# Attention's sums of a head: order of their products and their place ahead of the scores

## The chip, the core and the metric

The kernel runs on one core of one Trainium2 chip. The metric is the device time of one execution in microseconds. Engines are named as the profile names them: PE (TensorE matmuls), PEld (its weight loads), DVE (VectorE), ACT (ScalarE), POOL (GpSimd) and SP (SyncE, which issues the transfers). Each engine executes its own instructions in the order in which the built program has them, and waits for others by semaphores.

## What is computed

The reference is one block: a conditioned layer norm, attention with a compressive memory over four segments of 512 tokens, a second conditioned layer norm, and a token-mixing MLP. Attention, cut to what matters here, for each of 32 heads of 32 numbers:

```
for s in range(4):                       # segments of 512 tokens
    logits = qs @ ks.T * 32**-0.5 + causal_mask
    p = softmax(logits)
    a_dot = p @ vs
    a_mem = (phi(qs) @ M) / (phi(qs) @ z + 1e-6)
    o = g * a_mem + (1 - g) * a_dot
    M += phi(ks).T @ vs ; z += sum(phi(ks))
```

with `g = sigmoid(beta)`. Then `x + ga * (o @ wo)`, the norm, and the MLP over the token axis. All is in float32.

## The kernel before, in words

Float32 accuracy comes from splitting numbers into a first part (rounded) and a second part (the rest), and multiplying parts: a projection has three products for each pair of tiles.

Attention goes over 32 **units** (line 364): two passes, in each eight groups of four heads, in each two segments. A unit has four heads, so there are 128 heads in this count; number n is unit n // 4, head n % 4. For a unit:

- `project` (line 380) makes keys, values and queries (tiles `nps`, lines 188 to 197, and `qps`, lines 199 to 203), transposes keys (`kps`, line 415) and sends the split operands of each head to the tiles `sk` by SP's transfers.
- `memory` (line 446) reads the compressive memory (`rd`, line 455) and updates it (`up`, line 465).
- `maxima(t, h)` (line 473) computes scores in three matmul groups `sx`, `sy`, `sz` (line 483) into two banks, takes row maxima on DVE (line 485), and after each second head transposes them (`nmps`, line 491); four small transfers (line 498) put them as rows into `sk`.
- `scores(t, h)` (line 512) computes transposed scores, less the maxima, in four matmuls `a0`, `a1`, `a2` (two; lines 519, 522, 525, 526) into two banks. ACT takes the exponential of each bank (lines 520, 523, 527) into `p32`, of which there are two buffers. POOL masks the diagonal blocks (line 530), ACT rounds all 1280 columns to float16 as the probabilities' **first part** (line 532), and POOL subtracts it from `p32` in two halves of 640 columns, which gives the **second part** (line 534). Both parts lie in `ph`, of which there are two buffers.
- `values(t, h)` (line 536) sums over keys: ten products with the first part, 97 columns wide, then ten with the second part, 65 wide, all into the one bank `pv` (line 548). DVE takes the reciprocal of the row sums (551), adds the three column groups (553) and scales (555); POOL adds the memory's part in all but the first segment (558). After the fourth head PE transposes the unit's result (`ops`, line 563), ACT copies it out and SP stores it.

The loop at line 690 emits, for step n, the scores of head n, the maxima of head n + 3, the sums of head n - 1, a piece of the projection eight steps ahead, and planned work of other kinds. This is not the order that runs: the program is built with a scheduler (line 1138) that places the instructions of each engine by its own timing estimate, with the order of emission as their priority. Which instruction of PE follows which is therefore a result of the build. PE's order was read off the built programs before and after.

`norm_all` (line 214) normalizes four token tiles, twice at the start. Its means, variances and factors lie in a small tile `mv4` of 20 numbers for each partition. `csb` (line 104) holds the condition vector `c` and its sigmoid, 16 numbers for each partition, and is not read after line 110.

Of the kernel before, what the change touches and what calls it, by code (L numbers as in the profile page):

```python
# [7 lines left out]
F32 = mybir.dt.float32  # L8
# [10 lines left out]
P = 128  # L19
# [8 lines left out]
NV = 97  # L28
# [3 lines left out]
VL = 1  # L32
# [12 lines left out]
def attention_and_mlp(ctx, tc, x, wq, wkv, wo, beta, w1, b1, w2, b2, c, wm_a, wm_b, out):  # L45
# [19 lines left out]
    a = par.__enter__()  # L65
    scb, gaw = (a.tile([P, D], F32, name=n) for n in ("scb", "gaw"))
    acst_pool = tc.tile_pool(name="acst", bufs=1)
    acst = acst_pool.__enter__()
# [6 lines left out]
    def bank(tag, bufs, name):  # L75
        return psum.tile([P, 512], F32, tag=tag, bufs=bufs, name=name)
# [27 lines left out]
    csb = acst.tile([P, 2, NK], F32, name="csb")  # L104
# [39 lines left out]
    def new_page(name):  # L144
        return page.tile([P, 2, 512], F32R, tag="page", bufs=16, name=name)
# [32 lines left out]
    def load_w(g, pr):  # L178
        res = W[pr, g] = {}
        for kind, part in (("v", 0), ("v", 1), ("q", 0)):  # L180
            load_part(g, pr, kind, part, res)
        if pr == 0:
            keep_w(g)
# [30 lines left out]
    def norm_all(tiles):  # L214

        with tc.high_priority():
            m = acst.tile([P, 5, 4], F32, tag="mv4", bufs=1, name="mv4")
            r, t, nb = m[:, 2], m[:, 3], m[:, 4]
            mv = m[:, 0:2].rearrange("p a b -> p (a b)").rearrange("p (i a) -> p i a", a=2)
            for k, src in enumerate(tiles):  # L220
                st = const.tile([P, 2, 6], F32, tag="st", bufs=4, name="st")
                for i in range(2):
                    V.bn_stats(st[:, i], src[:, 512 * i:512 * i + 512])
                last_stats = V.bn_aggr(mv[:, k], st)
            A.activation(r, mv[:, :, 1], AF.Ln, bias=eps)
            exp = A.activation(r, r, AF.Exp, scale=-0.5)
            V.scalar_tensor_tensor(t, mv[:, :, 1], EPS, r, op0=ALU.add, op1=ALU.mult)
            V.scalar_tensor_tensor(t, t, -0.5, r, op0=ALU.mult, op1=ALU.mult)
            V.scalar_tensor_tensor(r, t, 1.5, r, op0=ALU.add, op1=ALU.mult)
            V.scalar_tensor_tensor(nb, mv[:, :, 0], -1.0, r, op0=ALU.mult, op1=ALU.mult)  # L230
            for k, src in enumerate(tiles):
                if k % 2:
                    last_v = V.tensor_scalar(src, src, r[:, k:k + 1], nb[:, k:k + 1], op0=ALU.mult, op1=ALU.add)
                else:
                    last_a = A.activation(src, src, AF.Identity, scale=r[:, k:k + 1], bias=nb[:, k:k + 1])
        return last_stats, exp, last_a, last_v
# [85 lines left out]
    for i in range(2):  # L322
        ps = bank("s2", 2, f"scps{i}")
        for j in range(4):
            T.transpose(ps[:, 128 * j:128 * j + 128], bc[:, 4 * i + j], ident)
        A.copy(scb[:, 512 * i:512 * i + 512], ps)
    last_stats = norm_all(xs[0])[0]
    srow.append(scale_row(1))
    for cb in range(2):
# [16 lines left out]
    b = late.__enter__()  # L346
# [12 lines left out]
    def reload_h(seg, ct):  # L359
        pg = new_page(f"h{seg}_{ct}")  # L360
        SY.dma_start(pg.bitcast(F32), hT1[seg - 2, ct])
        hpages[seg, ct] = pg
# [140 lines left out]
    @contextmanager  # L503
    def behind(n, engines):

        with ExitStack() as s:
            for e in engines:
                if (n, e) in marks:
                    s.enter_context(tc.issue_after(marks[n, e].ins))
            yield  # L510
# [25 lines left out]
    def values(t, h):  # L536
        pr, g, seg = its[t]
        d = st[t]
        am, ph = d["am"], d["ph", h]
        pv = bank("pv", 1, f"pv{t}_{h}").rearrange("p (a n) -> p a n", a=4)  # L540
        col = {0: lambda i: 128 * i, 1: lambda i: 512 + 128 * (i - 1), 2: lambda i: 1024 + 128 * (i - 2),
               3: lambda i: 896}
        n = 0
        for part, w in ((0, NV), (1, 65)):
            for i in range(4):
                for j in range(i + 1):
                    o = col[j](i)
                    T.matmul(pv[:, i, 0:w], ph[:, part, o:o + 128], d["vp"][:, j, h, 0:w], start=(n == 0),  # L548
                             stop=(n == 19), skip_group_check=True)
                    n += 1  # L550
        V.reciprocal(pv[:, :, 0], pv[:, :, 0])
        red = r_.tile([P, 4, 32], F32, tag="red", bufs=2, name=f"red{t}_{h}")
        V.tensor_reduce(red, pv[:, :, 1:97].rearrange("p a (c e) -> p a e c", c=3), axis=AX.X, op=ALU.add)
        ah = am[:, :, 32 * h:32 * h + 32]
        V.scalar_tensor_tensor(red if seg else ah, red, gate[:, 1, 4 * g + h:4 * g + h + 1],  # L555
                               pv[:, :, 0:1].to_broadcast([P, 4, 32]), op0=ALU.mult, op1=ALU.mult)
        if seg:
            G.tensor_tensor(ah, ah, red, op=ALU.add)
        if h < 3:
            return  # L560
        ps = bank("ms", 1, f"ops{t}")
        for i in range(4):
            T.transpose(ps[:, 128 * i:128 * i + 128], am[:, i], ident)
        ot = r_.tile([P, L], F32, tag="ot", bufs=1, name=f"ot{t}")
        A.copy(ot, ps)
        SY.dma_start(oT[g, :, L * seg:L * seg + L], ot)
        del st[t]
# [29 lines left out]
    def at(f, n):  # L597
        if 0 <= n < 4 * NI:
            f(n // 4, n % 4)
# [3 lines left out]
    def seg_load(seg):  # L603
        seg_x[seg] = [load_x(s2p, tt) for tt in range(4 * seg, 4 * seg + 4)]
        return norm_all(seg_x[seg])
# [69 lines left out]
    for g in range(2, NG):  # L675
        n = 8 * g - 13
# [5 lines left out]
    for j in range(32):  # L682
        n = ML0 + MLS * j
        later(n, lambda j=j: mod_fetch(j), n + 2, lambda r, j=j: mod_late(j, r), "V")
    plan(WO0 - 3, lambda: spread(gaw, 0))
    for i in range(8):
        n = WO0 + WOS * i
        later(n, lambda i=i: wo_fetch(i), n + 2, lambda r, i=i: wo_split(i, r), "G")

    for n in range(-LEADS, 4 * NI + VL):  # L690
        at(scores, n)
        at(maxima, n + LEADS)
        at(values, n - VL)
        m = n + LEADP
        if 0 <= m + 4 < 4 * NI:
            t = (m + 4) // 4
            if its[t][:2] not in W:
                with tc.issue_after(last_sk[0, 3].ins):
                    load_w(its[t][1], its[t][0])
        if m >= 8:  # L700
            at(project, m)
        if 59 <= m < 67:
            seg, ct = 2 + (m - 59) // 4, 2 * ((m - 59) % 4)
            reload_h(seg, ct)
            reload_h(seg, ct + 1)
        if 4 * NI - 5 <= m < 4 * NI + 3:
            i = m - 4 * NI + 5
            for c in (2 * (i % 4), 2 * (i % 4) + 1):
                wop[c, i // 4] = new_page(f"wo{c}_{i // 4}")
                if c < 5 or i < 4:  # L710
                    SY.dma_start(wop[c, i // 4].bitcast(F32), wos[c, i // 4])
        for f, engines in todo.pop(n, ()):
            with behind(n, engines):
                f()
# [14 lines left out]
    w = cw_pool.__enter__()  # L729
# [412 lines left out]
```

## Time and profile before

| | |
|---|---|
| median of 3 runs | 2239.49 us (2235.74 to 2240.94) |
| the profiled execution's own time | 2239.78 us |
| its span in the profile | 2238.1 us |
| DVE, ACT busy | 75%, 51% of the span |
| DMA | 423.05 MB, 189 GB/s in the mean |

The span runs from the first to the last profiled instruction of the program. A busy share is the union of an engine's instructions over the span; PE's matmuls overlap each other, so their durations are longer than the distance from one start to the next, and a price for PE's time has to be taken from the distances. In the grouped view a row gives line, engine, operation, tiles and shapes, the count, busy us and mean ns, then the engine's idle time just before and what ended it.

### The profile page before, as it was taken

What the parts mean: (1) busy time and instruction counts of PE and PEld (TensorE: products, weight loads), DVE (VectorE), ACT (ScalarE), POOL (GpSimd) and SP (SyncE); (2) the same over time, 40 slices, a digit from 0 to 9 for tenths busy, and PEclk for the clock granted to TensorE, in tenths of its full rate; (3) what the DMA queues carried; (4) which work ended last, traced back from release to release, by engine and by line L of the source; (5) the groups of instructions that cost most, each with busy time, mean ns of one, the idle gap of its engine ahead of it and who ended that gap; (6) DMA issues with size and microseconds to landing.
All of it is one profiled execution on the core that took longest, in us unless ns stands there. A gap on an engine that the chain in (4) does not pass through costs nothing.

```text
span 2238.1 us, 38277 instructions
## 1 busy us (share of the span) xinstructions
PE 2199.5 (98%) x13786; PEld 1888.4 (84%) x13786; DVE 1679.5 (75%) x3762; ACT 1137.1 (51%) x2082; POOL 731.0 (33%) x831
## 2 busy tenths in 40 slices
PE   8999999998999999999999999999999999999999
PEld 5889898888999899988888888888888888888887
DVE  7677677766777777655758766888888896869687
ACT  5477777665666666655546633533334242424232
POOL 2176656656777676654001200033330000000000
PEclk9999999999999999999999999999999999999999
DMA  7556565687566565665664587655556541414134
GB/s 285 189 175 206 162 188 156 182 298 239 158 195 194 159 202 181 197 185 181 230 209 154 224 324 264 257 206 224 205 201 235 201 147 58 155 57 146 57 123 151
DMA packets 175185, 423.05 MB, mean 189 GB/s; under 512 B 17524, under 2 KB 71828, under 8 KB 166036
## 3 DMA queue, kind: packets, MB, share of 16 engines
q1 hardware_dynamic: 174996, 420.61, 56.8%
q8 instruction: 109, 1.79, 0.3%
q14 instruction: 80, 0.66, 0.1%
HBM read 244.62 MB, written 125.06 MB: 165 GB/s over the span
## 4 chain that ended last, share of the span: by engine, by line
PE 85%; DMA 4%; POOL 3%; DVE 3%; ACT 3%; issue 2%; SPq 1%; ACTq 0%; DVEq 0%; POOLq 0%
PE mx L922 48%; PE nps L195 10%; PE po L792 8%; PE qps L203 7%; PE pv L548 3%; POOL ph L534 2%; PE a L519 1%; PE sz L483 1%; PE sx L483 1%; DMA sk<-sg 1%; ACT ph L532 1%; PE a L522 1%; DVE wv L125 1%; DMA sk<-nt 1%; PE srow L296 1%
## 5 line engine op out<-in xcount | busy, mean ns | idle before, releaser
L922 PE MATMUL mx<-bU,sp 128*128 128x512 f32 x2352 | 534.4, 389 | 0.9 <-DVE ac L929 0.9
L922 PEld LDWEIGHTS mx<-bU,sp 128*128 128x128 f32 x2352 | 441.3, 188 | 93.5 <-issue 1.3
L195 PE MATMUL nps<-wv,h 128*128 128x256 f32 x3072 | 441.7, 283 | 1.2 <-DVE h L125 0.5
L534 POOL TENSOR_TENSOR ph<-p,ph 128x640 f16<-128x640 f32 x256 | 382.3, 1514 | 157.1 <-ACT ph L532 154.2
L122 ACT CAST sp<-wr 128x384 fp32r<-128x384 f32 (+2 forms) x408 | 217.0, 545 | 423.6 <-PE mx L922 352.1
L922 PE MATMUL mx<-bA,sp 128*128 128x512 f32 x1764 | 430.5, 389 | 0.0
L195 PEld LDWEIGHTS nps<-wv,h 128*128 128x128 f32 x3072 | 407.1, 189 | 8.8 <-DVE h L125 2.0
L922 PEld LDWEIGHTS mx<-bA,sp 128*128 128x128 f32 x1764 | 331.2, 188 | 68.6
L125 DVE TENSOR_TENSOR sp<-wr,sp 128x384 fp32r<-128x384 f32 (+2 forms) x408 | 259.6, 647 | 28.6 <-ACT sp L122 28.4
L929 DVE TENSOR_TENSOR ac<-mx,ac 128x512 f32<-128x512 f32 x280 | 189.4, 685 | 84.1 <-PE mx L922 83.1
L203 PE MATMUL qps<-h,wq 128*128 128x512 f32 x768 | 201.7, 403 | 0.2
L532 ACT CAST ph<-p 128x1280 f16<-128x1280 f32 x128 | 161.3, 1260 | 42.6 <-POOL p L530 42.1
L792 PE MATMUL po<-wo,ots 128*128 128x512 f32 x768 | 179.4, 390 | 0.0
L792 PEld LDWEIGHTS po<-wo,ots 128*128 128x128 f32 x768 | 143.3, 188 | 29.0 <-DVE x L795 0.2
L203 PEld LDWEIGHTS qps<-h,wq 128*128 128x128 f32 x768 | 141.9, 191 | 29.5 <-ACT vp L406 0.9
L922 PE MATMUL mx<-bB,sp 128*128 128x512 f32 x588 | 164.0, 389 | 0.0
L530 POOL TENSOR_SCALAR_AFFINE_SELECT p<-p 128x256 f32<-128x256 f32 x256 | 123.5, 493 | 99.7 <-ACT p L527 51.6
L548 PE MATMUL pv<-vp,ph 128*128 128x97 bf16 (+1 forms) x2560 | 143.7, 203 | 2.0 <-DVE red L555 1.0
L548 PEld LDWEIGHTS <-ph 128*128 128x128 f16 x2560 | 115.8, 99 | 25.8 <-issue 10.8
L485 DVE CUSTOM_DVE_ANT_0 sx<-sx,mask 128x128 f32<-128x128 f32 (+1 forms) x256 | 93.6, 366 | 48.5 <-PE sx L483 46.6
L922 PEld LDWEIGHTS mx<-bB,sp 128*128 128x128 f32 x588 | 110.4, 188 | 22.9
L929 DVE TENSOR_TENSOR cc<-mx,cc 128x512 f32<-128x512 f32 x140 | 94.8, 683 | 37.6 <-PE mx L922 37.5
(207 smaller groups left out, 3164.2 us busy)
## 6 DMA issues: line engine op xcount, KB each, us to landing
sk<-sg SPq DMA_DIRECT2D x384, 128.0 KB
wr<-in_w_dram SPq DMA_DIRECT2D x28, 1024.0 KB
wr<-in_w_dram SPq DMA_DIRECT2D x32, 768.0 KB
bstu<-ucd SPq DMA_DIRECT2D x28, 768.0 KB
wsp<-wv SPq DMA_DIRECT2D x32, 512.0 KB
rawm<-in_wm_b_dram SPq DMA_DIRECT2D x32, 512.0 KB
wv<-wsp SPq DMA_DIRECT2D x32, 512.0 KB
pcd<-cc SPq DMA_DIRECT2D x14, 1024.0 KB
```

Source lines behind the costliest of these rows:

```text
L122: last_hi[0] = A.copy(hi, src)
L125: return lo_eng.tensor_tensor(lo, src, hi.bitcast(F32), op=ALU.subtract)
L195: T.matmul(ps[:, aa], h[:, j, 128 * tt:128 * tt + 128], wt[:, i, o:o + 256], start=(n == 0), stop=(n >= 6 * NK - 2), skip_group_check=True)
L203: T.matmul(ps, wt[:, i, o:o + 128], h[:, j], start=(k + n == 0), stop=(3 * k + n == 3 * NK - 1))
L485: marks[4 * t + h - LEADS, "V"] = V.tensor_tensor_reduce(o, o, mask[:, 384 - 128 * i:], 1.0, -3.0e38, op0=ALU.add, op1=ALU.max, accum_out= ...
L530: G.affine_select(w, w, pattern=[[0, 2], [1, 128]], compare_op=ALU.is_ge, fill=0.0, base=0, channel_multiplier=-1)
L532: marks[n, "A"] = A.copy(ph[:, 0], p32)
L534: marks[n, "G"] = G.tensor_tensor(ph[:, 1, c], p32[:, c], ph[:, 0, c], op=ALU.subtract)
L548: T.matmul(pv[:, i, 0:w], ph[:, part, o:o + 128], d["vp"][:, j, h, 0:w], start=(n == 0), stop=(n == 19), skip_group_check=True)
L792: T.matmul(ps, os_[:, i, P * ct:P * ct + P], wop[ct, nh][:, j], start=(n == 0), stop=(n == 3 * NK - 1))
L922: T.matmul(ps, ops[q][:, i, P * k:P * k + P], b[:, j], start=(m == 0 and first), stop=(m == 3 * nk - 1), skip_group_check=True)
L929: V.tensor_tensor(d, ps, d, op=ALU.add)
```

## The change

Three edits:

1. `values` multiplies the second parts first, then the first parts, and goes through the blocks backwards.
2. The loop emits the sums of head n - 1 ahead of the scores of head n and the maxima of head n + 3, so that they have the higher priority in the scheduler.
3. `norm_all` keeps its numbers in `csb`, whose contents are no longer needed then, in place of a tile of its own. `nb` takes the place of `t`.

```diff
     def norm_all(tiles):
 
         with tc.high_priority():
-            m = acst.tile([P, 5, 4], F32, tag="mv4", bufs=1, name="mv4")
-            r, t, nb = m[:, 2], m[:, 3], m[:, 4]
-            mv = m[:, 0:2].rearrange("p a b -> p (a b)").rearrange("p (i a) -> p i a", a=2)
+            flat = csb.rearrange("p a k -> p (a k)")
+            r, t = flat[:, 8:12], flat[:, 12:16]
+            nb = t
+            mv = flat[:, 0:8].rearrange("p (i a) -> p i a", a=2)
...
         n = 0
-        for part, w in ((0, NV), (1, 65)):
-            for i in range(4):
-                for j in range(i + 1):
+        for part, w in ((1, 65), (0, NV)):
+            for i in range(4)[::-1]:
+                for j in range(i + 1)[::-1]:
                     o = col[j](i)
                     T.matmul(pv[:, i, 0:w], ph[:, part, o:o + 128], d["vp"][:, j, h, 0:w], start=(n == 0),
                              stop=(n == 19), skip_group_check=True)
...
     for n in range(-LEADS, 4 * NI + VL):
+        at(values, n - VL)
         at(scores, n)
         at(maxima, n + LEADS)
-        at(values, n - VL)
```

The first edit adds one line, so a line of the attention is one higher in the profile after: the products stand at L549, POOL's second part at L535.

In the built program the twenty products of a head, which before stood in pieces between other matmuls for most heads, stand as one run for nearly all of them.

## The prediction

> **What bounds the kernel now.** I read the page first, for the span and the busy shares, then the busy time of the stage in which attention runs.
>
> ```profile
> span 2238.1 us, 38277 instructions
> PE 2199.5 (98%) x13786; PEld 1888.4 (84%) x13786; DVE 1679.5 (75%) x3762; ACT 1137.1 (51%) x2082; POOL 731.0 (33%) x831
> PE 85%; DMA 4%; POOL 3%; DVE 3%; ACT 3%; issue 2%; SPq 1%; ACTq 0%; DVEq 0%; POOLq 0%
> ```
>
> ```profile
> 100.00:1040.00 940.00, 917.21 (x7957) 833.19 (x7956) 671.74 (x1970) 625.72 (x1136) 610.77 (x709) 0.99 0.63 192
> ```
>
> The columns of this stage's row are its ends and length, then busy PE, PEld, DVE, ACT and POOL, the granted clock, and DMA. PE (TensorE) is the bound: 98% of the span, and most of the chain that ended last. Attention runs from 100 to 1040 us, and PE is idle there for 940.0 - 917.2 = 22.8 us; that is all an order without waits could save. POOL (GpSimd) is busy 65% and ACT 67% of that stage, so each keeps up only while its work is spread evenly between PE's.
>
> The next view groups instructions by line within that stage: busy time, mean ns of one, then idle time and what ended it.
>
> ```profile
> L527 ACT ACTIVATE p<-a,shift 128x384 f32<-128x384 f32 x128 | 74.6, 583 | 55.0 <-PE a L526 53.9
> L530 POOL TENSOR_SCALAR_AFFINE_SELECT p<-p 128x256 f32<-128x256 f32 x256 | 123.5, 493 | 99.7 <-ACT p L527 51.6 <-ACT p L523 46.3 <-PE sy L483 1.3
> L532 ACT CAST ph<-p 128x1280 f16<-128x1280 f32 x128 | 161.3, 1260 | 42.6 <-POOL p L530 42.1
> L534 POOL TENSOR_TENSOR ph<-p,ph 128x640 f16<-128x640 f32 x254 | 379.5, 1515 | 155.7 <-ACT ph L532 152.9 <-DVE mx L485 2.6
> L548 PE MATMUL pv<-vp,ph 128*128 128x97 bf16 x2531 | 142.5, 203 | 2.0 <-DVE red L555 1.0 <-POOL ph L534 0.9
> L548 PEld LDWEIGHTS <-ph 128*128 128x128 f16 x2532 | 114.8, 99 | 25.6 <-issue 10.8 <-POOL ph L534 1.9 <-ACT ph L532 1.1
> ```
>
> A head's probabilities pass from PE to ACT (exponential, L527), POOL (mask, L530), ACT (first part, L532), POOL (second part, two halves, L534) and back to PE (L548). PE hardly waits for it today: 0.9 us in matmuls and 1.9 us in weight loads over the 128 heads.
>
> **The chain's length.** The timeline of a head for which no engine had a queue (start, length, then idle time before and what ended it):
>
> ```profile
> 983.38 0.33 PE L526 MATMUL a<-sk 98*128 98x256 f32 x1
> 983.75 0.58 ACT L527 ACTIVATE p<-a,shift 128x384 f32<-128x384 f32 x1 [4.11 <-PE a L526]
> ...
> 984.40 0.41 POOL L530 TENSOR_SCALAR_AFFINE_SELECT p<-p 128x256 f32<-128x256 f32 x1 [2.40 <-ACT p L527]
> ...
> 984.84 1.26 ACT L532 CAST ph<-p 128x1280 f16<-128x1280 f32 x1 [0.51 <-POOL p L530]
> ...
> 986.18 2.77 POOL L534 TENSOR_TENSOR ph<-p,ph 128x640 f16<-128x640 f32 x2 [1.37 <-ACT ph L532]
> ```
>
> From the end of the last score matmul (983.71) the first part is ready at 986.10, after 2.4 us, and the second at 988.95, after 5.24 us. Each is a floor: a queue on POOL only adds. The sum of the grouped means agrees: 0.58 + 0.49 + 1.26 + 2 x 1.515 = 5.4 us.
>
> **The change part by part.** The same instructions run before and after on every engine, so only order and waits can move time. The first 580 of PE's instructions keep their order, and so do its last 5148 (the later products and the MLP): I cost those at nothing.
>
> *Norms' numbers in c's place.* Instructions and their order are the same; `nb` overwrites `t` on the same engine after its last read, and the second use waits for readers that it waited for before. Its cost lies between -0.2 and +0.5 us (half a microsecond is one instruction such as L530); I take 0.
>
> *Second parts first, one run.* Before, the ten products with the first part needed only the 2.4 us and were work for PE while POOL made the second part. Now the first product needs POOL's second half, and all twenty stand behind it, with all of PE's later work behind them. The work itself is as long in one run as in pieces. What matters is how much other PE work the built order has between a head's last score matmul and its first product with the second part. Prices per instruction are distances between starts in PE's timeline:
>
> ```profile
> 634.09 0.40 PE L483 MATMUL sx<-sk 96*128 96x128 f32 x2
> 634.32 0.52 PE L195 MATMUL nps<-wv,h 128*128 128x256 f32 x3
> 634.68 0.34 PE L483 MATMUL sy<-sk 96*128 96x384 f32 x1
> 634.86 1.92 PE L195 MATMUL nps<-wv,h 128*128 128x256 f32 x15
> 636.62 0.23 PE L525 MATMUL a<-sk 98*128 98x128 f32 x1
> 636.68 0.33 PE L526 MATMUL a<-sk 98*128 98x256 f32 x1
> 636.85 0.41 PE L195 MATMUL nps<-wv,h 128*128 128x256 f32 x2
> 637.10 0.40 PE L519 MATMUL a<-sk 98*128 98x512 f32 x1
> 637.34 0.76 PE L195 MATMUL nps<-wv,h 128*128 128x256 f32 x5
> ...
> 638.16 0.92 PE L548 MATMUL pv<-vp,ph 128*128 128x97 bf16 x20
> 638.92 0.42 PE L522 MATMUL a<-sk 98*128 98x384 f32 x1
> 639.18 0.39 PE L483 MATMUL sz<-sk 96*128 96x512 f32 x1
> 639.40 0.28 PE L195 MATMUL nps<-wv,h 128*128 128x256 f32 x1
> ```
>
> So a projection matmul is 0.118 us (634.86 to 636.62 for fifteen), `sx` 0.23, `sy` 0.18, `sz` 0.22, `a0` 0.24, `a1` 0.18 to 0.26, the `a2` pair 0.23, the run of twenty 0.76. Example, unit 22, head 3: between its `a2` and its products the changed order has two `rd` and four `up` (0.11 each by their width of 132), `sz`, `sx`, `a0`, `a1`, `sy`, the run of head 2, `sz`, `a2`, `sx`, `a0`, `sy`, `a1`: 3.8 us. The chain needs 5.24, so PE stands 1.5 us.
>
> Done for all 128 heads, **before** 5 fall short of 5.24 us, by 3.2 us in all, which fits the 0.9 + 1.9 us above. **After** 30 fall short, by 48.0 us; 28 of these are heads 2 and 3 of a unit. The worst are heads 2 and 3 of unit 12 (1.7 and 2.2 us of work), head 3 of 23 (2.6), heads 2 and 3 of 28 (2.6, 2.5) and heads 0 and 1 of 31, the last (2.0, 2.4). There the projections, which fill PE beside heads 0 and 1, have run out, and dependent scores, maxima and sums follow each other. Term one: 48 - 3 = **+45 us**. Ends: 30 if other waits lengthen the distances, 60 if POOL's queue lengthens the chain (3.8 us of POOL per head against about 2.4 us of PE work there).
>
> *What else stands close.* The transposes of a unit's result (L563) wait for DVE and, in later segments, POOL after the last product:
>
> ```profile
> L551 DVE RECIPROCAL pv<-pv 128x4 f32<-128x4 f32 x126 | 23.8, 189 | 53.7 <-PE pv L548 53.4
> L553 DVE TENSOR_REDUCE red<-pv 128x128 f32<-128x384 f32 x126 | 69.8, 554 | 6.4
> L555 DVE SCALAR_TENSOR_TENSOR red<-red,gate,pv 128x128 f32<-128x128 f32 x94 | 32.0, 341 | 1.0
> L558 POOL TENSOR_TENSOR am<-am,red 128x128 f32<-128x128 f32 x94 | 59.2, 630 | 36.0 <-DVE red L555 28.0 <-DVE rdd L457 6.2 <-PE nps L195 1.1
> ```
>
> That is 1.08 us in a first segment and 1.71 in others. In the changed order 12 of 32 units have only 0.2 to 0.7 us between (two had 0.9 before): six times about 0.6 and six times about 1.1, **+10 us**. In the same thin stretches scores and maxima follow within 0.2 to 0.7 us on banks that ACT (0.58 to 0.69 us) or DVE (0.37 to 0.70 us) must empty first; alone I count 37 us more of such shortage, but most lies under the wait for POOL: 0 to 37, I take **+10**. SP's queue is reordered by up to 22 places; the row transfers of the maxima keep at least 4.5 us of PE work before the scores that read them, so 0.
>
> *What goes.* The 22.8 us of idle PE have other causes for the most part (maxima, transfers), and longer waits give those time: 0 to -22.8; I take **-10**.
>
> *The clock.* After idle PE the granted clock (column before the DMA share) halves:
>
> ```profile
> 243.40:246.10 2.70, 0.71 (x5) 0.42 (x4) 2.70 (x6) 2.70 (x8) 2.67 (x4) 1.00 0.47 194
> 246.10:252.90 6.80, 6.25 (x38) 5.64 (x39) 4.37 (x16) 4.38 (x10) 3.15 (x3) 0.50 0.34 124
> 755.60:758.10 2.50, 0.37 (x4) 0.20 (x3) 1.69 (x8) 0.93 (x3) 2.41 (x5) 1.00 0.28 110
> 758.10:761.50 3.40, 3.40 (x28) 2.87 (x29) 0.62 (x2) 2.80 (x4) 0.71 (x2) 0.50 0.02 5
> ```
>
> About 2 us of idleness brought 3.4 or 6.8 us at half clock, 1.7 to 3.4 us lost. The new order makes some six places with as much idleness: six times 1.7 is **+10**; ends 0 and 20. The Trainium skill, "TensorE: Matmul & The Clock Gate", section "Why this matters for your kernels", says that the clock falls back only for gaps over about 3 us; by that rule this term is 0 and the sum 2295. The two rows above speak against it, as the clock fell after 2.0 and 2.1 us of idleness.
>
> Sum: 45 + 10 + 10 - 10 + 10 = +65 us on the profiled execution's 2239.8 us, which lies 0.3 us above the median of the runs shown (2239.5): **2305 us**.
>
> **The rivals.**
> *Mild:* waits replace each other. The products' wait takes its small value (30 - 3), all 22.8 us of today's idleness go into its shadow, the bank waits hide, and the clock stays up: 27 + 10 - 22.8 = +14, to 2254; with half of today's idleness left, 2265. For it: most shortages are in the same stretches. Against it: today's waits are spread over the whole stage.
> *Heavy:* heads 2 and 3 become bound by POOL throughout: 60 - 3 + 10 + 25 - 10 + 20 = +102, to 2342. For it: POOL's 3.8 us per head. Against it: heads 0 and 1 have over 6 us in every unit but the last.
> *Faster:* one run frees the sums' bank and the `ph` buffer at once, so exponentials start earlier and today's idleness goes: 2239.8 - 20 = 2220. It decides if the second part is ready within the work in front of it, that is if the chain took under 2.6 us; its first part alone takes 2.4, so the profile speaks against it.
> *The change does nothing:* the scheduler's order could have come out the same. It hasn't: PE's differs from instruction 581 on.
>
> **How the numbers follow.** Forecast, 60%; mild, 18%; heavy, 15%; faster, 5%; no difference, 2%. The range of 2254 to 2342 takes in the forecast's own ends, mild and the lower half of heavy. Within 0.2% (4.5 us) is about what a measurement of this kernel can't tell from no change; slower by more holds forecast, mild and heavy: 93%.
>
> **What would show it.** In the profile after, PE's idle time in attention grows from 22.8 to some 75 us, and the matmuls of the sums (L549 there) have idle time put down to POOL's L535, 30 us or more where 0.9 stood; the transposes (L564) show waits for L556 or L559; there are more spells at half clock. After 1100 us all is as before. I am wrong if that wait stays under 10 us, or if PE's idle time falls.

## The result

| | median | lowest to highest | runs |
|---|---|---|---|
| before | 2237.61 us | 2234.37 to 2240.94 | 4 |
| after | 2381.92 us | 2378.54 to 2387.09 | 4 |

The ratio is 1.0644 [1.063, 1.0658]: 144 us slower. The direction was forecast; the size, +65 us, was less than half of it, and the time lies above the range that ended at 2342. The profiled execution after took 2382.48 us.

From the page of the kernel after: span, busy time, the granted clock in 40 slices, and the engines' shares of the chain that ended last.

```profile
span 2380.8 us, 38252 instructions
PE 2264.2 (95%) x13786; PEld 1926.7 (81%) x13786; DVE 1682.7 (71%) x3762; ACT 1142.1 (48%) x2082; POOL 718.2 (30%) x831
PEclk9989999988999898998999999999999999999999
PE 80%; ACT 5%; DVE 5%; POOL 4%; DMA 4%; issue 1%; SPq 1%; ACTq 0%; DVEq 0%; POOLq 0%
```

The work is the same: as many matmuls, and DVE, ACT and POOL busy within 13 us of before. Two things about PE differ. It is idle for 116.6 us of the span where it was idle for 38.6, and it is *busy* 64.7 us longer on the same 13786 matmuls. The granted clock, counted below, accounts for this second half.

The windows of both kernels show where. The first row of each is attention, from 100 us to the last transpose of a unit's result; the second is the rest. The columns are ends and length, busy PE, PEld, DVE, ACT and POOL, clock, DMA share and GB/s. Before:

```profile
100.00:1054.10 954.10, 931.31 (x8045) 844.88 (x8044) 676.49 (x1982) 627.80 (x1138) 614.43 (x713) 0.99 0.63 191
1054.10:2238.10 1184.00, 1179.34 (x5200) 975.53 (x5198) 931.97 (x1617) 462.69 (x860) 99.66 (x64) 1.00 0.51 182
```

After:

```profile
100.00:1208.50 1108.50, 1007.99 (x8095) 893.18 (x8094) 682.77 (x1989) 633.56 (x1139) 602.43 (x713) 0.92 0.56 166
1208.50:2380.80 1172.30, 1167.38 (x5148) 965.50 (x5146) 928.72 (x1610) 461.70 (x858) 98.91 (x64) 1.00 0.51 182
```

Attention took 154.4 us more. The rest took 11.7 us less because 52 of its matmuls moved into attention: at 1184.00 / 5200 = 0.228 us each they make 11.8 us. That leaves 142.7 us, the growth of the span. PE's idle time in attention rose from 22.8 to 100.5 us, by **77.7 us**. The mean clock fell from 0.99 to 0.92, and the records of the clock have only full and half speed, so about 2 x 0.08 x 1108.5 = 177 us ran at half clock. Counted out spell by spell it is 25 spells with 177.5 us after and four with 20.5 us before. PE was busy for 146.9 us of the former and 18.0 us of the latter, and half of that busy time is lost: (146.9 - 18.0) / 2 = **64.5 us**. The two terms make 142.2 of the 142.7 us; e1 and e2 below show that the match is this close because two smaller effects cancel.

What PE waited for within attention after (total us, times, longest us):

```profile
PE sx L484 <- DMA sk<-sg: 24.9, 10, 6.8
PE pv L549 <- POOL ph L535: 23.0, 15, 2.2
PE kps L416 <- ACT vp L407: 8.6, 16, 1.4
PE sy L484 <- DVE mx L486: 7.1, 17, 0.8
PE a L523 <- ACT p L528: 5.8, 7, 1.8
PE a L526 <- ACT p L521: 5.0, 7, 1.3
```

The forecast wait of the sums (`pv`) for POOL is there with 23.0 us, less than the 30 us that the prediction named as its sign. The longest row is one that the prediction did not have: the maxima's first matmul (`sx`) waits for the transfer that brings the next unit's queries and keys to `sk`, 24.9 us against this row before:

```profile
PE sx L483 <- DMA sk<-sg: 6.9, 3, 5.3
```

A thin stretch in PE's timeline after (start, length, then idle time and what ended it), heads 2 and 3 of a unit for which no projection is left:

```profile
942.73 0.31 PE L526 MATMUL a<-sk 98*128 98x128 f32 x1
942.87 0.33 PE L527 MATMUL a<-sk 98*128 98x256 f32 x1
943.04 0.40 PE L484 MATMUL sz<-sk 96*128 96x512 f32 x1
943.28 0.40 PE L520 MATMUL a<-sk 98*128 98x512 f32 x1
943.52 0.40 PE L484 MATMUL sx<-sk 96*128 96x128 f32 x2
944.29 0.44 PE L484 MATMUL sy<-sk 96*128 96x384 f32 x1 [0.38 <-DVE mx L486]
944.57 0.33 PE L523 MATMUL a<-sk 98*128 98x384 f32 x1
946.62 1.55 PE L549 MATMUL pv<-vp,ph 128*128 128x65 bf16 x20 [1.72 <-POOL ph L535]
947.96 0.46 PE L526 MATMUL a<-sk 98*128 98x128 f32 x1
948.21 0.52 PE L527 MATMUL a<-sk 98*128 98x256 f32 x1
949.24 1.12 PE L416 MATMUL kps<-ident,k 128*128 128x128 f32 x4 [0.51 <-ACT vp L407]
950.01 6.68 PE L203 MATMUL qps<-h,wq 128*128 128x512 f32 x22
```

From the `a2` pair (942.73) to its sums there are six matmuls of other heads, and PE stands for 0.38 and 1.72 us. Then the twenty products take 1.55 us instead of the 0.92 us quoted from before. What follows is slower too, the dense query projections (`qps`) among it. The windows around this place:

```profile
942.80:946.20 3.40, 1.73 (x10) 1.12 (x8) 1.41 (x5) 1.34 (x4) 2.92 (x4) 1.00 0.82 228
946.20:953.00 6.80, 5.87 (x33) 5.00 (x34) 0.74 (x1) 3.33 (x6) 4.78 (x8) 0.50 1.03 315
953.00:980.30 27.30, 24.79 (x222) 22.65 (x222) 18.57 (x62) 13.82 (x25) 11.89 (x16) 1.00 0.50 134
```

PE was busy for 1.73 of 3.40 us at full clock, and the next 6.8 us ran at half. So 1.67 us of idleness (the piece of 1.72 us reaches over the window's end) cost a further 5.87 / 2 = 2.9 us, half of the time in which PE then worked. The groups of the projections show this over all of attention (count, busy us, mean ns): before, then after.

```profile
L203 PE MATMUL qps<-h,wq 128*128 128x512 f32 x696 | 181.2, 404 | 0.1
```

```profile
L203 PE MATMUL qps<-h,wq 128*128 128x512 f32 x696 | 196.7, 438 | 0.0
L549 PE MATMUL pv<-vp,ph 128*128 128x65 bf16 (+1 forms) x2560 | 131.7, 210 | 27.7 <-POOL ph L535 23.0 <-DVE am L556 2.6 <-DVE red L556 1.6
L564 PE MATMUL ops<-ident,am 128*128 128x128 f32 x128 | 23.2, 311 | 6.3 <-POOL am L559 3.7 <-DVE am L556 2.6
```

The `qps` have no idle time of their own in either kernel and yet take 15.5 us more: they pay for the waits ahead of them. Durations of matmuls overlap, so this row shows the direction and not the loss.

### The profile page after: what moved, and what is told of

It reads as the page before. It is cut to its first block, busy times and chain, and to the rows that moved or that the text cites. A ratio compares the mean times of both kernels' runs of the same rounds, so it can differ in the third digit from the quotient of the medians.

```text
span 2380.8 us, 38252 instructions
## 1 busy us (share of the span) xinstructions
PE 2264.2 (95%) x13786; PEld 1926.7 (81%) x13786; DVE 1682.7 (71%) x3762; ACT 1142.1 (48%) x2082; POOL 718.2 (30%) x831
## 4 chain that ended last, share of the span: by engine, by line
PE 80%; ACT 5%; DVE 5%; POOL 4%; DMA 4%; issue 1%; SPq 1%; ACTq 0%; DVEq 0%; POOLq 0%
PE mx L923 45%; PE nps L195 10%; PE po L793 8%; PE qps L203 7%; POOL ph L535 3%; PE pv L549 3%; DMA sk<-sg 2%; ACT ph L533 2%; PE kps L416 1%; ACT p L521 1%; PE sz L484 1%; PE a L520 1%; PE sx L484 1%; DMA sk<-nt 1%; PE srow L297 1%
## 5 line engine op out<-in xcount | busy, mean ns | idle before, releaser
L195 PE MATMUL nps<-wv,h 128*128 128x256 f32 x3072 | 424.5, 282 | 1.9 <-DVE h L125 0.7
L535 POOL TENSOR_TENSOR ph<-p,ph 128x640 f16<-128x640 f32 x256 | 375.3, 1488 | 132.7 <-ACT ph L533 132.5
L195 PEld LDWEIGHTS nps<-wv,h 128*128 128x128 f32 x3072 | 397.6, 189 | 12.4 <-DVE h L125 2.0
L203 PE MATMUL qps<-h,wq 128*128 128x512 f32 x768 | 217.0, 434 | 0.1
L203 PEld LDWEIGHTS qps<-h,wq 128*128 128x128 f32 x768 | 159.2, 214 | 33.1 <-ACT vp L407 0.4
L549 PE MATMUL pv<-vp,ph 128*128 128x65 bf16 (+1 forms) x2560 | 131.7, 210 | 27.7 <-POOL ph L535 23.0
L549 PEld LDWEIGHTS <-ph 128*128 128x128 f16 x2560 | 112.8, 103 | 46.2 <-POOL ph L535 31.2
L521 ACT ACTIVATE p<-a,shift 128x512 f32<-128x512 f32 x128 | 88.3, 690 | 103.1 <-PE a L520 56.5
```

What stands on the lines that cost most here:

```text
L195: T.matmul(ps[:, aa], h[:, j, 128 * tt:128 * tt + 128], wt[:, i, o:o + 256], start=(n == 0), stop=(n >= 6 * NK - 2), skip_group_check=True)
L203: T.matmul(ps, wt[:, i, o:o + 128], h[:, j], start=(k + n == 0), stop=(3 * k + n == 3 * NK - 1))
L521: A.activation(p32[:, 0:512], b0, AF.Exp, scale=SCALE, bias=shift)
L535: marks[n, "G"] = G.tensor_tensor(ph[:, 1, c], p32[:, c], ph[:, 0, c], op=ALU.subtract)
```

## The experiments

Two questions were open. Which of the three edits does it? And is the clock's fall a matter of one long gap (theory G) or of the idle share of a stretch of 3.41 us (theory W)? That length is read off the records: the spells at half clock in the kernel after last 3.41, 6.83, 10.24 or 20.48 us. For the first, theory A said that it is the place of the sums in the loop, theory B that it is the order of the products, which makes the run wait for POOL's second half. When A held, it split: A1, the sums' place ahead of the *maxima*; A2, their place ahead of the *scores*.

In the table, "short" is what the prediction's ledger, its count head by head, gives for the built order of PE: heads with under 5.24 us of PE work between their last score and their first product with the second part, and by how much in all.

| loop order | products | short: heads, us | ratio |
|---|---|---|---|
| before: scores, maxima, values | before | 5, 3.2 | 1 |
| after: values, scores, maxima | changed | 30, 48.0 | 1.0644 [1.063, 1.0658] |
| e1_loop: values, scores, maxima | before | 31, 41.2 | 1.0583 [1.0566, 1.0599] |
| e5_mid: scores, values, maxima | before | 29, 38.8 | 1.0499 [1.0482, 1.0516] |
| e2_parts: scores, maxima, values | changed | 3, 1.3 | 0.9985 [0.9976, 0.9995] |
| e4_maxfirst: maxima, scores, values | before | 3, 0.9 | 0.9972 [0.996, 0.9983] |
| e10_mvs: maxima, values, scores | before | 4, 1.2 | 0.9983 [0.9974, 0.9992] |
| e6_mvs_all: maxima, values, scores | changed | 3, 1.0 | 0.9981 [0.9971, 0.9992] |
| e7_mf_all: maxima, scores, values | changed | 2, 0.6 | 0.9997 [0.9988, 1.0007] |

After, e6 and e7 also have the norms' edit. All "short" numbers rest on one price that is too low, as told in the part on why the prediction was right and wrong; counted again with a higher one they fall, and the two groups stay as far apart.

### e1_loop: the loop's order alone

```diff
+        at(values, n - VL)
         at(scores, n)
         at(maxima, n + LEADS)
-        at(values, n - VL)
```

> The loop's order alone (sums of the last head emitted ahead of scores and maxima); products keep the first parts first, norms keep their own tile. Theory A, the priority of the sums bunches the projections beside heads 0 and 1 and leaves heads 2 and 3 without cover, whatever the products' order: 31 heads have under 5.24 us of work before their second parts, as in the whole change, so +90 to +145 us (2330 to 2385), with 15 or more spells at half clock. Theory B, the wait of all twenty products for the second part is what costs: the ten products with the first part are cover again, so at most +30 us (2270).

2371.36 us (2366.38 to 2374.7). The row of attention:

```profile
100.00:1206.90 1106.90, 1024.47 (x8144) 901.20 (x8143) 700.53 (x2009) 637.99 (x1151) 603.70 (x713) 0.93 0.55 168
```

The loop's order alone brings 1.0583 of 1.0644: PE idle for 82.4 us, 20 spells at half clock. Its largest waits in attention:

```profile
PE pv L548 <- POOL ph L534: 20.5, 23, 1.9
PE sx L483 <- DMA sk<-sg: 14.3, 8, 7.4
PE pv L548 <- ACT ph L532: 7.0, 9, 1.3
```

Here the first parts come first, and the sums wait for POOL almost as long as after (20.5 and 23.0 us): ten products are too little cover where nothing else is left. Theory A holds, B falls. Idle time (+59.6 us) and half clock ((124.4 - 18.0) / 2 = 53.2 us) account for 112.8 of the 130.9 us by which the span grew. The other 18 us are not accounted for; most of them are busy time of PE that the clock does not explain. PE's time in attention falls into 136 busy pieces here and into 42 before. In e8 below a burst of two matmuls counts as busy for 0.73 us and each further matmul adds only 0.23, so each burst has some 0.27 us on top; 94 more of them would make 25 us. That is an estimate, not shown by a run.

### e2_parts: the products' order alone

```diff
-        for part, w in ((0, NV), (1, 65)):
-            for i in range(4):
-                for j in range(i + 1):
+        for part, w in ((1, 65), (0, NV)):
+            for i in range(4)[::-1]:
+                for j in range(i + 1)[::-1]:
```

> The products' order alone (second parts first, blocks backwards, one run); the loop and the norms as before. Theory A: only 3 heads have under 5.24 us of work before their products, so no loss: -10 to +5 us (2228 to 2243). Theory B: every head waits for the second part ahead of all twenty products: +60 to +140 us (2300 to 2380).

2236.92 us (2232.86 to 2240.91), no slower than before.

```profile
100.00:1056.90 956.90, 930.21 (x8070) 846.72 (x8069) 674.13 (x1987) 626.51 (x1140) 603.88 (x713) 0.99 0.62 191
```

PE's idle time in attention is 26.7 us where 22.8 stood. With the old loop the scheduler puts the one run where the second part is ready: the sums wait for POOL for 0.6 us in all. The products themselves keep PE busy for less time in one run; this row is of before, then of e2:

```profile
L548 PE MATMUL pv<-vp,ph 128*128 128x97 bf16 (+1 forms) x2560 | 143.7, 203 | 2.0 <-DVE red L555 1.0 <-POOL ph L534 0.9
L548 PE MATMUL pv<-vp,ph 128*128 128x65 bf16 (+1 forms) x2560 | 124.2, 201 | 1.6 <-DVE red L555 1.0 <-POOL ph L534 0.6
```

Over the whole span PE is busy for 2192.9 us in e2 and 2199.5 before. Here more idle time takes most of that gain back. With half of the busy time at low clock taken off, 2190.5 us are left before, 2183.0 in e2, 2207.0 in e1 and 2190.7 after. So the changed products' order takes 7.5 us off with the old loop and 16.3 with the new one, and the new loop adds 16.5 with the old products. After has both, and that is why idle time and clock alone seem to make up its whole loss.

### e3_norm: the norms' numbers alone

```diff
-            m = acst.tile([P, 5, 4], F32, tag="mv4", bufs=1, name="mv4")
+            flat = csb.rearrange("p a k -> p (a k)")
...
```

> The norms' numbers in c's place alone. Every engine's order of attention is that of the kernel before. Both theories: 0, within 4 us (2234 to 2242). If it moved by more, addresses or waits at the start would have a part in the loss.

2237.01 us (2234.78 to 2242.49), ratio 0.9992 [0.9982, 1.0002]: nothing that can be told from zero.

### e4_maxfirst: maxima ahead of the scores, sums last

```diff
+        at(maxima, n + LEADS)
         at(scores, n)
-        at(maxima, n + LEADS)
         at(values, n - VL)
```

> The loop emits maxima, then scores, then sums (sums last, as before); products and norms as before. Theory A: the sums have the lowest of the three priorities, 3 heads fall short of 5.24 us: -15 to +10 us (2223 to 2248). Theory C, any change of the order of emission upsets a scheduler's lucky order: +50 us or more (2290).

2233.76 us (2231.86 to 2235.45), ratio 0.9972 [0.996, 0.9983].

```profile
100.00:1047.00 947.00, 927.04 (x8047) 841.73 (x8046) 668.56 (x1982) 628.22 (x1138) 611.98 (x713) 0.99 0.63 192
```

If a later place of the maxima costs time, an earlier one might save some. It does: idle time 20.0 us instead of 22.8, and two spells at half clock, 10.2 us, instead of four with 20.5. The wait of `sx` for `sk`, 6.9 us before, is 0.7 us here.

### e5_mid: the sums ahead of the maxima, behind the scores

```diff
         at(scores, n)
-        at(maxima, n + LEADS)
         at(values, n - VL)
+        at(maxima, n + LEADS)
```

> The kernel before with the loop emitting scores, then sums, then maxima: the sums pass the maxima alone, not the scores; products and norms as before. Theory A1, what bunches the projections is that the sums come ahead of the maxima: 29 heads have under 5.24 us of work before their second parts (38.8 us short in all), so +90 to +140 us (2330 to 2380). Theory A2, it is that they come ahead of the next head's scores: within 15 us of before (2225 to 2255).

2353.0 us (2350.11 to 2354.49), ratio 1.0499 [1.0482, 1.0516].

```profile
100.00:1178.90 1078.90, 1004.60 (x8090) 885.08 (x8089) 679.35 (x1989) 630.54 (x1140) 603.05 (x713) 0.94 0.57 171
```

Idle time 74.3 us, 18 spells at half clock. One exchange of two neighbours in the loop brings 112 of the 144 us, and the scores still come ahead of the sums. A1 holds, A2 falls as the main cause; the step from 1.0499 to e1's 1.0583 is what the place ahead of the scores adds once the maxima stand last. As in e1, idle time (+51.5 us) and half clock ((107.2 - 18.0) / 2 = 44.6 us) leave 18 us of the span's growth open.

### e6_mvs_all: the whole change, but with the maxima first

```diff
+        at(maxima, n + LEADS)
+        at(values, n - VL)
         at(scores, n)
-        at(maxima, n + LEADS)
-        at(values, n - VL)
```

with the products' and the norms' edits of the change.

> All of the change, but the loop emits maxima, then sums, then scores: the sums stand ahead of the next head's scores and behind the maxima. Theory A1: 3 heads fall short, by 1.0 us in all, so -15 to +10 us (2225 to 2250). Theory A2: +100 to +145 us (2340 to 2385).

2235.76 us (2232.05 to 2241.25), ratio 0.9981 [0.9971, 0.9992].

```profile
100.00:1055.00 955.00, 926.02 (x8073) 842.89 (x8072) 674.37 (x1987) 626.05 (x1138) 605.37 (x713) 0.99 0.64 191
```

The counterpart: second parts first, one run, ahead of the next head's scores, as the change says, and nothing is lost. Only the maxima stand elsewhere.

### e7_mf_all: e4's loop with the other two edits

```diff
+        at(maxima, n + LEADS)
         at(scores, n)
-        at(maxima, n + LEADS)
         at(values, n - VL)
```

with the products' and the norms' edits of the change.

> Second parts first in one run and the norms in c's place, with the loop emitting maxima, scores, sums. Theory A1: the gains of the products' order alone (-0.15%) and of maxima first alone (-0.28%) add: 2225 to 2236 us. Rival: both gains are the same idle time, then 2230 to 2240 us.

2239.28 us (2236.5 to 2241.73), ratio 0.9997 [0.9988, 1.0007]. The gain that was expected did not come: the small gains of e2 and e4 do not add. Attention took 960.3 us with 31.9 us of idle PE, though its ledger is the shortest of all (2 heads, 0.6 us). At this size the ledger of one wait no longer ranks the orders.

### e8_clock: what halves the clock

A kernel of its own, which leaves out the reference's whole computation. In each of 18 stretches 64 dense matmuls of 128x512 are followed for some 34 us by bursts of m such matmuls; between two bursts PE waits for one, two or four of ACT's copies.

```
for cols, chain, m in SECTIONS:
    ...
    for k in range(n):
        ...
        for i in range(m):
            T.matmul(ps, w, r, start=True, stop=True)
        src = ps
        for c in range(chain - 1):
            A.copy(s[c % 2], src)
            src = s[c % 2]
        A.copy(r[:, 0:cols], src[:, 0:cols])
```

> No attention at all: it leaves out the whole computation. 18 stretches of some 34 us, each behind 64 matmuls without a wait, in which PE has bursts of 2 to 18 matmuls of 128x512 and between them waits for a chain of one, two or four copies on ACT (gaps of about 0.9, 1.6 and 2.8 us). Theory W, the clock goes by the busy share of each stretch of 3.41 us: it halves wherever PE is idle for over some 1.3 to 1.6 us of 3.41 (a share under about 0.55 to 0.6), with gaps of 0.9 us too. Theory G, the clock goes by the length of a gap: stretches with gaps of 0.9 and 1.6 us keep the full clock at any share.

It ran once (1004.33 us). The repeated gaps were 0.73, 1.38 and 2.68 us long. The table gives PE's idle time in 3.41 us, worked out from the gap and the length of a burst at full clock, and how long the clock was half in each stretch:

| gap | fell | did not fall |
|---|---|---|
| 0.73 us | m=2 (1.71 us idle): 37.0 of 40.8 us | m=3 (1.47) and more |
| 1.38 us | m=3 (2.00): 37.3 of 40.0; m=4 (1.82): 33.6 of 40.8; m=5 (1.67): 34.9 of 42.2 | m=6 (1.55) and more |
| 2.68 us | all six, from m=5 (2.22): 34.0 of 37.6, to m=14 (1.48) and m=18 (1.29): 3.4 of 29.6 and of 27.2 | |

Rows of four stretches; the columns are ends and length, busy PE, PEld, ACT and POOL, clock, DMA share and GB/s. They are m=2 and 3 with a gap of 0.73 us, m=5 and 6 with 1.38:

```profile
22.80:63.50 40.70, 25.36 (x44) 10.41 (x44) 12.31 (x21) 0.00 (x0) 0.55 0.00 0
83.70:115.20 31.50, 18.31 (x57) 9.23 (x57) 10.55 (x18) 0.00 (x0) 1.00 0.00 1
452.70:494.90 42.20, 26.77 (x60) 15.98 (x60) 13.23 (x22) 0.00 (x0) 0.59 0.00 1
514.80:546.80 32.00, 18.26 (x66) 11.53 (x66) 12.03 (x20) 0.00 (x0) 1.00 0.00 1
```

The first two differ in one matmul for each burst and not in the gap, as PE's timeline shows for m=2, still at full clock:

```profile
24.24 0.73 PE L42 MATMUL ps<-r,w 128*128 128x512 f32 x2 [0.73 <-ACT r L47]
25.70 0.73 PE L42 MATMUL ps<-r,w 128*128 128x512 f32 x2 [0.73 <-ACT r L47]
...
85.40 0.96 PE L42 MATMUL ps<-r,w 128*128 128x512 f32 x3 [0.73 <-ACT r L47]
```

(the last line is of m=3). The same gap of 0.73 us halves the clock or does not, by the work between. Theory G falls: the clock does not go by the length of a gap. Theory W holds in that the work within a short stretch decides, but not with a sharp bound on the idle time. Every change of the clock in e8 lies a whole number of 3.41 us after the first one. In stretches cut at these times, the least idle time that led to a fall was 1.59 us, and the longest that did not was 1.83. Two of them, the first followed by half clock and the second not:

```profile
23.15:26.56 3.41, 1.82 (x6) 0.60 (x4) 1.21 (x3) 0.00 (x0) 1.00 0.00 0
535.15:538.56 3.41, 1.65 (x6) 1.05 (x6) 1.55 (x4) 0.00 (x0) 1.00 0.00 0
```

In the attention kernels the bound on the idle time lies lower still. Cut in the same way, 9 of the 25 falls after followed stretches with under 1.6 us of idleness, and so did 13 of 20 in e1 and 10 of 18 in e5. The one with the least in the kernel after, 0.67 us, and the spell behind it:

```profile
1110.00:1113.40 3.40, 2.73 (x12) 1.48 (x10) 3.27 (x15) 2.50 (x4) 2.02 (x3) 1.00 0.79 169
1113.40:1123.70 10.30, 9.45 (x40) 7.13 (x40) 3.12 (x11) 4.83 (x6) 7.63 (x10) 0.50 0.75 275
```

The profile counts a short burst as busy for longer than its columns take (0.73 us for two matmuls, 0.23 for each further one), so the columns that the started matmuls move are a better count. In e8 no stretch that led to a fall has more than 3072 columns (six matmuls of 512) and none of the others fewer. In the kernel after, all 25 falls have at most 3561, and of the 247 other stretches at full clock all but two have 3584 or more. In e5 it separates less well: there the falls reach 3594, and six of the others have fewer. This count was made on traces that were there already; no run was built to test it.

### e9_mf_norm: e4's loop and the norms' edit

```diff
+        at(maxima, n + LEADS)
         at(scores, n)
-        at(maxima, n + LEADS)
         at(values, n - VL)
```

with the norms' edit of the change.

> Maxima, scores, sums in the loop, and the norms in c's place; first parts first as before. PE's order is that of e4_maxfirst. If that kernel's gain of 0.28% is real: ratio 0.996 to 0.998 again (2230 to 2236 us). If it was chance between chips: ratio 0.999 to 1.001.

2232.12 us (2231.83 to 2234.09), ratio 0.9969 [0.9957, 0.9981]: e4's gain a second time (its order on PE is that of e4), and the fastest version of the study, 0.3% below before and 6.3% below after (2232.12 / 2381.92 = 0.937, measured at different times).

### e10_mvs: e6's loop alone

```diff
+        at(maxima, n + LEADS)
+        at(values, n - VL)
         at(scores, n)
-        at(maxima, n + LEADS)
-        at(values, n - VL)
```

> The loop emits maxima, sums, scores; products and norms as before. Theory A1 (only a place ahead of the maxima bunches the projections): 4 heads fall short, by 1.2 us, so -10 to +8 us (2230 to 2247). Theory A2 (a place ahead of the next head's scores costs when the first parts come first): +90 us or more (2330).

2234.86 us (2232.91 to 2239.07), ratio 0.9983 [0.9974, 0.9992]. Sums ahead of the next head's scores cost nothing as long as they stand behind the maxima: A1 with the products' old order too. One reading is left beside A1. In both loop orders that lost (values, scores, maxima and scores, values, maxima) the maxima come last of the three, and in the three that did not they stand earlier. The order values, maxima, scores would tell the two readings apart; it was not run.

## Why the prediction was right and wrong

**The bound, right.** PE was the bound, and attention the only stage that lost, though it lasted to 1208 us and not the 1100 named; behind it a matmul still costs 0.228 us (1172.30 / 5148).

**The norms at 0, right:** e3, 0.9992 [0.9982, 1.0002].

**The built order, right; the edit that it was charged to, wrong.** The ledger (30 heads short, 28 of them heads 2 and 3) found the place: in every order with 29 to 31 short heads the time rose by 5 to 6%, and in every order with 2 to 5 its ratio lay between 0.997 and 1.000. But the prediction put it under "second parts first, one run". That edit alone makes 3 heads short and no loss (e2). What empties the stretches is the place of the sums ahead of the maxima (e5), or that the maxima come last, which these orders don't separate. By the records of PE, of which some are missing, each unit before has 2.6 us of projections in the mean between the sums of head 2 and head 3; after it has 0.6, e5 0.9, and e4 and e6, which lost nothing, 2.5 to 2.6. The projections run out beside heads 0 and 1, and the maxima (`sz`) lie 29 to 32 us of PE work ahead of the scores (`a0`) that use them instead of 22 to 24.

**The sums' wait at +45, too large alone.** 27.7 us of idleness stand before the `pv` matmuls, 25.7 more than before. One price was too low. `rd` and `up` stand as two records for each matmul of the kernel, so that the four `up` here take 0.97 us, 0.24 each and not 0.11:

```profile
609.12 1.13 PE L465 MATMUL up<-v,pk 128*128 128x132 f32 x8
610.09 0.52 PE L548 MATMUL pv<-vp,ph 128*128 128x97 bf16 x11
```

The example of unit 22, with two `rd` and four `up`, then has some 4.6 us of work and not 3.8. Counted again from the order of PE's records after, with 0.22 for each of them and prices near the prediction's for the others, some 27 heads fall short, by 39 us; e1 has 27 and 37 us, e5 26 and 33, and the orders that did not lose 2 to 4 with at most 2.4. The claim that the work is as long in one run as in pieces was wrong too: e2's products take 124.2 us where 143.7 stood.

**Transposes at +10:** 6.3 us (L564).

**Bank waits at +10:** 5.8 + 5.0 + 7.1 = 17.9 us in the three rows shown, 1.9 before.

**Not in the sum:** the transposes of the keys (`kps`) wait for ACT for 8.6 us where 0.6 stood.

**Today's idleness at -10, wrong in sign:** the `sx` wait for `sk` was to hide and grew by 18.0 us. The ledger counted the work ahead of the products and not the work ahead of the next unit's first maxima; where projections have run out, PE reaches those before the transfers have landed, 6.8 us in the worst case. The transfers may be late as well: the first of each head's three on SP waited for PE's scores (L520) for 22.7 us in all, 5.5 before. The two were not separated.

Together the four terms came to +55, and PE's idle time grew by 77.7 us. They were 23 us too small, and that they came this near is partly luck, as one piece was too large and others were too small or missing.

**The clock at +10: this step failed.** That idleness of some 2 us brings 3.4 or 6.8 us at half clock was read rightly from the two places shown, and so was the price of 1.7 us for each 3.4. The count was wrong: "some six places with as much idleness" against 25 spells, 21 more than before. The spells last 177.5 / 25 = 7.1 us in the mean, with PE busy for most of it. So the term was 64.5 us instead of 10, and its upper end, 20, kept the range too low. Part of the reason is that 2 us of idleness was too high a mark: 14 of the 25 falls came after stretches of 3.41 us with less. The prediction had numbers that pointed there. Its 48 us of shortage in 30 heads is 1.6 us a head, with the transposes' and banks' waits in the same stretches on top; e8 and the count of columns, though, came only later. With 64.5 in place of 10 its sum would have been 2239.8 + 45 + 10 + 10 - 10 + 64.5 = 2359, and the 23 us of idleness missing from the first four terms are the rest.

**The page's rule, not borne out here.** The Trainium skill, "TensorE: Matmul & The Clock Gate", section "Why this matters for your kernels", advises "No PE-idle gaps >~3µs between matmul bursts". In e8 the clock fell with gaps of 0.73 us, and in the timeline above after one of 1.72 us. That the clock falls only for longer gaps, as the prediction put the rule, is therefore wrong in this case. The prediction rightly went by its rows.

**The rivals.** *Heavy* had nearly the right idleness (+82 before its clock term of 20, measured 77.7) for a reason that was not the cause: not POOL's pace alone (23.0 us) but many different waits in the same places. Its 3.8 us of POOL for each head are 3.9 by the rows shown ((123.5 + 379.5) / 128). *Mild* failed as its waits did not replace each other. *Faster*, through earlier exponentials, did not come; e2's 0.9985 is the most that the products' order gave without the loop's edit.

**What stays open.** Why the scheduler, with the sums' priority above that of the maxima, uses up the projections beside heads 0 and 1: only built orders were compared, and its own timing estimates were not examined. Whether it is the sums ahead of the maxima or the maxima in the last place: the order values, maxima, scores is missing. The half clock's 64.5 us are an account from the trace, which e8 supports but no run took away by itself. The 18 us of e1 and e5 have only an estimate.

## What to carry to other kernels

Where a scheduler takes the order of emission as priority, an exchange of two lines is a change of the whole built order: count, stretch by stretch, how much independent work lies ahead of each dependent group, of the next unit's inputs as well as of this unit's results, and keep what feeds later heads (here the maxima) ahead of what only finishes earlier ones. Price a thin stretch twice: its idle time, and, if the clock falls, half of the busy time that follows until PE is dense again; here the two were 77.7 and 64.5 us. Judge whether it falls by how many columns PE's matmuls move in 3.41 us (it did at up to 3072 in e8 and 3561 after), and not by the longest gap.

## What the runs showed of the hardware

The clock does not need one gap of some length. Gaps of 0.73 us halve it if PE's work between them is as short (e8, m=2: from 3.8 us on), and gaps of 1.38 us do not if six matmuls of 512 columns stand between them. Once low it can stay low: at m=2 for 37.0 of 40.8 us, in which PE is busy for 25.36 of 40.70 us, since the same matmuls then take longer. In the stretches of 3.41 us in which it came back, PE had been idle for 0.60 us or less in e8 and 0.40 or less in the kernel after; that alone did not bring it back, as it also stayed low after stretches with 0.16 us. In the kernel itself these 3.40 us with 1.24 us of idleness and 4224 columns kept the full clock, where 0.67 us and 3456 columns (above) did not:

```profile
437.60:441.00 3.40, 2.16 (x17) 1.95 (x17) 0.98 (x7) 0.89 (x2) 0.62 (x1) 1.00 0.37 93
```
